# Attention and a mixture of experts in one kernel: one put group for each list, score tiles filled ahead, the block for late rows laid out differently

## The chip, the core and the metric

The kernel runs on one core of a Trainium2 chip. The metric is the device time of one execution in microseconds. Five engines work side by side, each through its own queue of instructions in order: TensorE (PE; its weight loads are shown apart as PEld), VectorE (DVE), ScalarE (ACT), GpSimd (POOL) and SyncE (SP), which here only starts transfers. An engine waits for another one by semaphores.

## The reference

Windowed attention over 8 batches, 8 heads, 576 positions and 64 dimensions gives 4608 rows of 512. Each row then goes to two of eight experts, chosen by noisy gate logits.

```python
scores = scale * np.matmul(q, k.transpose(0, 1, 3, 2))
mask = (rel >= 0) & (rel < window)            # window = 64
scores = np.where(mask, scores, -1000000000.0)
attn = softmax(scores);  x = np.matmul(attn, v)       # rows of 512

logits = x @ w_gate;  noise_scale = np.log1p(np.exp(x @ w_noise))
noisy_logits = logits + noise_scale * noise
top2 = np.argpartition(-noisy_logits, 2, axis=1)[:, :2]
...
for e in range(8):
    for k in range(2):
        mask = top2[:, k] == e
        h = np.maximum(x[mask] @ w1[e], 0.0)          # 512 x 1024
        out[mask] += top2_w[mask, k, None] * (h @ w2[e])
```

(The softmax is written out in the original; `softmax` stands for it here.)

## The kernel before, in words

**Attention, the first 170 us.** 36 units j: nine blocks of 64 positions times four pairs of batches. Units 0 to 3 are the first block, which has no block before it. The loop over j is a pipeline written by hand: in iteration j stand the scores of unit j (L295, later L293), the softmax of j, the transposes of unit j-1 (L329) and the product with v of unit j-2 (L352). The softmax needs a tile `t` of 128 x 512. For later units ScalarE copies scores into it (L303); for units 0 to 3 GpSimd fills it with -8e9 (L305), in `soft_a(j)`. VectorE then copies the permitted scores over it (`soft_max`, L311), takes the maximum (L316), GpSimd subtracts it (L317), and ScalarE takes the exponential (L321). There is one PSUM tile for scores, so the scores of the next unit wait for the copy of this one. Ahead of the loop GpSimd and VectorE build constants (L161 to L596; VectorE's L439 to L596 read some of GpSimd's). `warm(n)` (L150) issues n matmuls on a constant tile whose result nobody reads; the first four units issue four each.

**Lists.** Expert 0 works on all its rows in a simple way. For each expert e from 1 to 7 the generator `top_list(e)` (L639) makes the list of slots: small VectorE steps, three products `tcc` (L670), and then marks and puts. A mark (L682) writes 128 x 512 ones and zeros that tell which lane a row goes to, nine of them for 36 columns. A put (L676) is a matmul of 128 x 50 in bf16 with a mark's columns as weights, 36 for a list, all into one PSUM tile. Marks go through one buffer, `hot`, with room for eight columns, so there are five groups (8, 8, 8, 8, 4), and the puts of a group must be through before its buffer takes new marks. Behind the last put `topa`, `lts` and `ixs` (L694 to L711) are computed, which the gathers and scatters of expert e need.

**Experts.** Each expert has three chunks of rows (384, 448, 384). `up(e, c)` runs eight steps of 12 fp32r matmuls (L857 to L859) that each fill one of three PSUM banks in turn; ScalarE (`hh`, L863) and VectorE (`hl`, L871 and L873; in the last chunk also four `raw` steps, L884 to L887, and `sl`, L878) read the bank. `down(e, c)` (L924 to L926, L979 to L981) writes its rows into `yo`, of which there are three buffers, and GpSimd scatters them to the output with adding DMAs (L900). It also issues the gathers of coming rows (L769). `xy` (L783) has two buffers and holds gathered rows while they are transposed.

**The order of all this.** `spread` lays the side work out over the matmuls of a stage: each part of a list has a start and an end as shares of the stage. `drain(1)` takes one step of the open generators (`pending`), and `due` holds what is to be issued so many calls later. `have(e)` drains until list e is made. List 1 is drained in up(0, 1) and down(0, 1); list 2 in up and down of (0, 2) and in up(1, 0); list e+2 for e = 1 to 5 in down(e, 1), up(e, 2), down(e, 2) and the next chunk's up.

**Late rows.** An expert with more rows than its lists hold needs extra work, `late_rows` (L1256), in the program ahead of the last work item, up(7, 2). Each engine loads the count `nov` into a register (L1259) and branches on it (L1260). With this input the count is zero and the block isn't entered.

## Time and profile before

| | us |
|---|---|
| runs | 1022.56, 1020.47, 1022.13 (median 1022.13) |
| profiled execution | 1023.62 |
| its span | 1021.9 |
| PE busy in the span | 985.5 (96%) |
| DVE busy | 693.6 (68%) |
| POOL busy | 540.7 (53%) |
| ACT busy | 464.7 (45%) |
| mean granted TensorE clock | 0.995 of full speed |

The profiled execution's time is 1.7 us above its span: what lies before the first and behind the last instruction. The durations of instructions below come from this one execution. In a timeline row the first number is the start and the second the length, in us from the span's start; matmuls overlap, so the distance of two starts (the pitch) is what a matmul costs. A bracket at the end says how long the engine had stood idle and what ended it.

### The profile page before, as it was taken

To read this page: it belongs to the slowest core of one execution; us is meant where nothing else is said; L and a number is where in the kernel's file an instruction comes from. 1 tells how busy PE (TensorE), PEld (TensorE's weight loads), DVE (VectorE), ACT (ScalarE), POOL (GpSimd) and SP (SyncE) were. 2 spreads that over 40 slices of the span, in tenths; PEclk is the share of its full clock that TensorE was granted. 3 is DMA by queue.
4 is the path that set the end of the run, shared out by engine and by line. 5 is a ranking of instruction groups with operands and counts; after the bars stand their busy time and mean duration, and the time that the engine had idled before them with its cause. 6 is when DMAs were issued, how large, how long until landed. Compare 5 with 4: busy or idle time off the path is not lost.

```text
span 1021.9 us, 23842 instructions
## 1 busy us (share of the span) xinstructions
PE 985.5 (96%) x9253; PEld 895.1 (88%) x9253; DVE 693.6 (68%) x1716; ACT 464.7 (45%) x1141; POOL 540.7 (53%) x763
## 2 busy tenths in 40 slices
PE   8988989999999999999999999999999999999996
PEld 7776777887888999899999999999999999998995
DVE  6668878755676767766775777678667775467531
ACT  4877775421244435433543254434443543354431
POOL 4432231222776376747575757564667575667411
PEclk9999999999999999999999999999999999999998
DMA  9987897734155135423443334432453344352122
GB/s 326 285 252 219 263 306 275 275 72 100 42 140 113 46 60 132 98 68 63 113 98 87 57 92 99 108 54 81 99 122 55 95 97 109 57 127 52 35 35 31
DMA packets 60667, 123.62 MB, mean 121 GB/s; under 512 B 9728, under 2 KB 9856, under 8 KB 60416
## 3 DMA queue, kind: packets, MB, share of 16 engines
q1 hardware_dynamic: 40816, 83.18, 25.2%
q0 software_dynamic: 19728, 38.82, 21.5%
q8 instruction: 75, 1.23, 0.5%
q14 instruction: 48, 0.39, 0.1%
HBM read 81.59 MB, written 40.37 MB: 119 GB/s over the span
## 4 chain that ended last, share of the span: by engine, by line
PE 74%; DVE 11%; issue 5%; ACT 4%; DMA 4%; POOL 2%; another core or an unknown queue 0%; POOLq 0%; ACTq 0%; DVEq 0%
PE ps_u L857 10%; PE ps_u L859 10%; PE ps_u L858 10%; PE ps_d L924 7%; PE ps_d L925 7%; PE ps_d L926 7%; PE ps_d L979 4%; PE ps_d L981 4%; PE ps_d L980 4%; DMA xg<-xrows,ixs 3%; PE ps_o L352 2%; PE ps_s L293 2%; DVE hot L682 1%; DVE t L311 1%; DVE mx L316 1%
## 5 line engine op out<-in xcount | busy, mean ns | idle before, releaser
L769 POOL DMA_INDIRECT xg<-xrows,ixs x258 | 282.5, 1095 | 65.3 <-issue 52.8
L857 PE MATMUL ps_u<-xh,w1h 128*128 128x384 f32 (+2 forms) x752 | 258.3, 343 | 1.5 <-PEq L1260 1.5
L859 PE MATMUL ps_u<-xh,w1l 128*128 128x384 f32 (+2 forms) x752 | 255.4, 340 | 0.0
L858 PE MATMUL ps_u<-xl,w1h 128*128 128x384 f32 (+2 forms) x752 | 255.4, 340 | 0.0
L863 ACT ACTIVATE hh<-ps_u 128x384 fp32r<-128x384 f32 x188 | 91.7, 488 | 149.6 <-PE ps_u L859 115.4
L900 POOL DMA_INDIRECT out_dram<-yo,lts x67 | 110.9, 1655 | 82.2 <-DVE yo L974 43.0
L857 PEld LDWEIGHTS ps_u<-xh,w1h 128*128 128x128 f32 x752 | 141.2, 188 | 3.5 <-ACT yo L971 1.7
L858 PEld LDWEIGHTS ps_u<-xl,w1h 128*128 128x128 f32 x752 | 141.3, 188 | 1.8
L859 PEld LDWEIGHTS ps_u<-xh,w1l 128*128 128x128 f32 x752 | 141.1, 188 | 1.4
L924 PE MATMUL ps_d<-w2h,hh 128*128 128x512 f32 x352 | 139.2, 395 | 0.6 <-ACT hh L863 0.6
L925 PE MATMUL ps_d<-w2l,hh 128*128 128x512 f32 x352 | 137.6, 391 | 0.3 <-issue 0.3
L926 PE MATMUL ps_d<-w2h,hl 128*128 128x512 f32 x352 | 137.8, 391 | 0.0
L873 DVE SCALAR_TENSOR_TENSOR hl<-ps_u,hh 128x384 fp32r<-128x384 f32 x132 | 73.3, 555 | 94.3 <-ACT hh L863 71.6
L871 DVE SCALAR_TENSOR_TENSOR hl<-ps_u,hh 128x256 fp32r<-128x256 f32 x56 | 23.8, 425 | 106.2 <-ACT raw L869 98.0
L888 ACT ACTIVATE sh<-raw 128x512 fp32r<-128x512 f32 x56 | 35.4, 632 | 128.3 <-DVE raw L887 104.8
L317 POOL TENSOR_TENSOR t<-t,mx 128x512 f32<-128x512 f32 x36 | 37.5, 1043 | 97.8 <-DVE mx L316 73.3
L926 PEld LDWEIGHTS ps_d<-w2h,hl 128*128 128x128 f32 x352 | 66.1, 188 | 14.5 <-DVE hl L873 0.3
L924 PEld LDWEIGHTS ps_d<-w2h,hh 128*128 128x128 f32 x352 | 66.3, 188 | 12.5 <-ACT hh L863 1.0
L925 PEld LDWEIGHTS ps_d<-w2l,hh 128*128 128x128 f32 x352 | 66.2, 188 | 12.2 <-issue 0.7
L768 POOL COPY spacer<-hh 1x1 f32<-1x1 f32 x137 | 33.8, 246 | 69.2 <-ACT hh L863 50.7
L798 ACT ACTIVATE xh<-xy 128x512 fp32r<-128x512 f32 (+2 forms) x67 | 41.2, 615 | 57.7 <-DVE xy L783 52.0
L930 ACT ACTIVATE yo<-ps_d,lts 128x512 f32<-128x512 f32 x35 | 24.1, 689 | 86.4 <-PE ps_d L926 66.8
(277 smaller groups left out, 2068.3 us busy)
## 6 DMA issues: line engine op xcount, KB each, us to landing
stage<-in_w_dram SPq DMA_DIRECT2D x56, 512.0 KB
out_dram<-zero SPq DMA_DIRECT2D x40, 256.0 KB
vw<-in_vx_dram SPq DMA_DIRECT2D x36, 260.0 KB
qc<-in_qT_dram SPq DMA_DIRECT2D x36, 256.0 KB
KW<-in_kT_dram SPq DMA_DIRECT2D x36, 256.0 KB
xrows<-x SPq DMA_DIRECT2D x36, 256.0 KB
xg<-xrows,ixs POOLq DMA_INDIRECT x258
stage<-in_w_dram SPq DMA_DIRECT2D x8, 256.0 KB
```

The source lines that it names most:

```text
L769: nc.gpsimd.indirect_dma_start(out=XG[e, c, t // 4][:, t % 4, :], out_offset=None, in_=XQ[:(DUMP + seen.get((e, c), NT) * 128) * 4], in_of ...
L798: nc.scalar.activation(h, cur[q], AF.Copy)
L857: nc.tensor.matmul(p[:, :n], lhsT=w1h[:, k, fs], rhs=xh[:, k, :n], start=(k == 0), stop=False)
L858: nc.tensor.matmul(p[:, :n], lhsT=w1h[:, k, fs], rhs=xl[:, k, :n], start=False, stop=False)
L859: nc.tensor.matmul(p[:, :n], lhsT=w1l[:, k, fs], rhs=xh[:, k, :n], start=False, stop=(k == KD - 1))
L863: nc.scalar.activation(h, p[:, :main], AF.Relu)
L873: nc.vector.scalar_tensor_tensor(l, p[:, :main], 0.0, h.bitcast(F32), op0=OP.max, op1=OP.subtract)
L900: s = nc.gpsimd.indirect_dma_start(out=out[:DUMP + seen.get((e, c), NT) * 128], out_offset=bass.IndirectOffsetOnAxis(ap=slot(e, c, q)[:m, ...
L924: nc.tensor.matmul(p, lhsT=hh[f][:, sl], rhs=w2h[:, f, :], start=(f == 0), stop=False)
L925: nc.tensor.matmul(p, lhsT=hh[f][:, sl], rhs=w2l[:, f, :], start=False, stop=False)
L926: nc.tensor.matmul(p, lhsT=hl[f][:, sl], rhs=w2h[:, f, :], start=False, stop=(f == KF - 1))
L979: nc.tensor.matmul(p, lhsT=xh, rhs=yh, start=(fresh and i == 0), stop=False, skip_group_check=True)
```

## The change

Three things are edited.

1. **Lists.** The 36 puts of a list now stand in one group. List 1 has a tile of its own for all nine marks (`lone`). Lists 2 to 7 put their marks into five buffers (`marks`): two into `hot`, two into a buffer of `xy`, and two, two and one into the three `yo` buffers. List 2 is marked and put in up(1, 0). Lists 3 to 7 are marked in up(e, 2) with e = 1 to 5; `let`, `last_steps` and `all_done` place the group behind the seventh of its eight steps.
2. **First units.** The tiles `t` of units 0 and 1 are filled ahead of GpSimd's constants, those of units 2 and 3 one iteration ahead, ahead of the subtract of unit 1 and 2. Units 2 and 3 issue one `warm` matmul in place of four.
3. **Late rows.** The register load stands ahead of down(7, 1), and the `If` gets `preferred_fallthrough_block=False`.

```diff
@@ -176,6 +176,15 @@
     nc.vector.tensor_scalar(maskT[:, 1], maskT[:, 0], -1.0, 1.0, op0=OP.mult, op1=OP.add)
 
 
+    EMPTY = {}
+
+    def fill(j):
+        EMPTY[j] = wk.tile([128, 8, 64], F32, name="t")
+        nc.gpsimd.memset(EMPTY[j], -8e9)
+
+    for j in range(2):
+        fill(j)
+
     quarter = consts.tile([128, 1], F32)
     for g in range(4):
         nc.gpsimd.memset(quarter[32 * g:32 * g + 32], float(g))
@@ -296,13 +305,12 @@
                                          start=True, stop=True)
 
     def soft_a(j):
-        t = wk.tile([128, 8, 64], F32, name="t")
-        T[j] = t
         i = j // NP
         if i:
-            nc.scalar.activation(t, ST[j].rearrange("p u g c -> p (u g) c")[:, :, cur_cols(i)], AF.Copy)
+            T[j] = wk.tile([128, 8, 64], F32, name="t")
+            nc.scalar.activation(T[j], ST[j].rearrange("p u g c -> p (u g) c")[:, :, cur_cols(i)], AF.Copy)
         else:
-            nc.gpsimd.memset(t, -8e9)
+            T[j] = EMPTY.pop(j)
 
     def soft_max(j):
         t, p = T[j], ST.pop(j).rearrange("p u g c -> p (u g) c")
@@ -636,6 +644,31 @@
         yield lambda: nc.vector.tensor_reduce(novf[:, E:E + 1], novf[:, 0:E], op=OP.add, axis=AX.X)
         yield lambda: nc.vector.tensor_copy(nov, novf)
 
+    ready, done, LONE = {1}, set(), {}
+
+    def marks(e):
+        if e == 1:
+            return [(0, LONE["p"].tile([128, NT, 128], BF, name="lone"))]
+        x = [exa.tile([128, HALF, 128], BF, name="hot"),
+             exa.tile([128, 4, KD, 32], F32, name="xy", bufs=2).rearrange("p t k c -> p (t k c)")]
+        x += [EXB["p"].tile([128, DM], F32, name="yo", bufs=3) for _ in range(3)]
+        x[1:] = [y.bitcast(BF).rearrange("p (q c) -> p q c", c=128) for y in x[1:]]
+        return [(HALF * k, y) for k, y in enumerate(x)]
+
+    def last_steps(e):
+        return calls[0] >= ready_at[e] + 29
+
+    ready_at = {}
+
+    def let(e):
+        ready.add(e)
+        ready_at[e] = calls[0]
+
+    def all_done(e):
+        ready_at[e] = -100
+        while e not in done:
+            drain(1)
+
     def top_list(e):
         def new(name, shape, dt=F32):
             return gw.tile(shape, dt, name=name, bufs=1)
@@ -675,15 +708,25 @@
             for q in range(a, b):
                 nc.tensor.matmul(got, lhsT=t[:, q - a], rhs=cc[:, q].rearrange("p v k -> p (v k)"),
                                  start=(q == 0), stop=(q == NT - 1))
-        for a in range(0, NT, HALF):
-            b = min(NT, a + HALF)
-            t = exa.tile([128, HALF, 128], BF, name="hot")
-            for q in range(a, b, 4):
-                yield lambda t=t, a=a, q=q: nc.vector.tensor_tensor(
-                    t[:, q - a:q - a + 4], lane[:, None, :].to_broadcast([128, 4, 128]),
-                    ln[:, q:q + 4, None].to_broadcast([128, 4, 128]), op=OP.is_equal)
-            due.append((calls[0] + PUT, lambda t=t, a=a, b=b: put(t, a, b)))
-            yield PUT
+        while e not in ready:
+            yield 1
+        if e > 1:
+            yield 8
+        hot = marks(e)
+        for q in range(0, NT, 4):
+            t = next(x[:, q - a:q - a + 4] for a, x in reversed(hot) if a <= q)
+            yield lambda t=t, q=q: nc.vector.tensor_tensor(
+                t, lane[:, None, :].to_broadcast([128, 4, 128]),
+                ln[:, q:q + 4, None].to_broadcast([128, 4, 128]), op=OP.is_equal)
+        yield PUT if e > 1 else PUT * 3
+        while e > 1 and not last_steps(e):
+            yield 1
+
+        def all_put():
+            for (a, t), b in zip(hot, [a for a, _ in hot[1:]] + [NT]):
+                put(t, a, b)
+            done.add(e)
+        yield all_put
         yield 1
         if not ALL:
             ALL["lt"] = EXB["p"].tile([128, E - 1, HB, 2], I32, name="lts")
@@ -1108,6 +1151,8 @@
             REST[j]()
         on(flip, j - 4)
         on(soft_b, j - 1)
+        if 0 < j < NP - 1:
+            fill(j + 1)
         on(soft_a, j)
         for f in turned.get(j, ())[1:]:
             f()
@@ -1121,7 +1166,7 @@
         if j >= FROM:
             drain_slots(1, gath)
         if j < NP:
-            warm(WARM)
+            warm(WARM if j < 2 else 1)
         on(transp, j - 1)
         on(logits, j - 4)
         if j >= NT:
@@ -1256,8 +1301,7 @@
     def late_rows():
         with ExitStack() as oc:
             ov = oc.enter_context(tc.tile_pool(name="ov", bufs=1))
-            ntot = nc.values_load(nov[0:1, E:E + 1], min_val=0, max_val=2 * OVT)
-            with tc.If(ntot > 0):
+            with tc.If(over["n"] > 0, preferred_fallthrough_block=False):
                 pads()
                 slot_writes()
                 for e in range(E):
@@ -1266,7 +1310,7 @@
                     with tc.For_i(0, ne, 1) as k:
                         overflow(ov, e, k, base)
 
-    later = {}
+    later, over = {}, {}
     for n, (e, c) in enumerate(work):
         nxt = work[n + 1] if n + 1 < len(work) else None
         if not nxt:
@@ -1293,13 +1337,17 @@
         elif c == 1 and e:
             parts0.append((0.0, 0.6, mix_w2(e, 3)))
         if c == 0 and 0 < e < E - 1:
-            parts0.append((0.0, 1.0, [lambda: drain(1)] * 32 + [lambda: have(e + 1)]))
+            if e == 1:
+                let(2)
+            parts0.append((0.0, 1.0, [lambda: drain(1)] * 32 + [lambda: have(e + 1) if e > 1 else all_done(2)]))
         if n == 2:
             parts0.append((0.0, 0.95, gather(*nxt)))
         if last and e < E - 2:
             if e == 0:
                 pending.append(top_list(2))
-            parts0.append((0.0, 1.0, [lambda: drain(1)] * (22 if e else 32)))
+            if e:
+                let(e + 2)
+            parts0.append((0.0, 1.0, [lambda: drain(1)] * (32 if e else 28) + [lambda: all_done(e + 2)] * (e > 0)))
         parts = [(0.0, 1.0, side)] + parts0
         if nxt and n > 2:
             parts.append((0.05, 1.0, later.pop(nxt, None) or gather(*nxt)))
@@ -1318,6 +1366,8 @@
             parts.append((0.0, 0.8, [lambda t=t: zero_out(t) for t in range(*ZEROS[:2])]))
         if n == 1:
             load_w1(1)
+            lone = ExitStack()
+            LONE["p"] = lone.enter_context(tc.tile_pool(name="lone", bufs=1))
             parts.append((0.06, 1.0, [lambda: drain(2)] * 38 + [lambda: have(1)]))
         if n == 0:
             parts.append((0.0, 0.1, halves[SPLIT:]))
@@ -1328,16 +1378,21 @@
             pending.append(top_list(e + 2))
             parts.append((0.0, 1.0, [lambda: drain(1)] * 22))
         if last and e < E - 2:
-            parts.append((0.0, 1.0, [lambda: drain(1)] * (14 if e else 22)))
+            parts.append((0.0, 1.0, [lambda: drain(1)] * (14 if e else 0)))
         if c == 0 and e:
             parts.append((0.0, 1.0, [x for i in range(3) for x in mix_w2(e, i)]))
+        if n == 3:
+            parts.append((0.0, 1.0, [lambda: drain(1)] * 24 + [lambda: have(2)]))
         if 1 < n < len(work) - 2:
             g = gather(*work[n + 2])
             parts.append((0.15, 1.0, g[:SOON]))
             later[work[n + 2]] = g[SOON:]
+        if n == len(work) - 2:
+            over["n"] = nc.values_load(nov[0:1, E:E + 1], min_val=0, max_val=2 * OVT)
         spread(down(e, c), KF * len(tiles(e, c)) - 2 * paired(e, c), *parts)
         if n == 1:
             rt.close()
+            lone.close()
             MIX["p"] = ex.enter_context(tc.tile_pool(name="mix", bufs=1))
             for x in ("th", "tl"):
                 W2[x] = MIX["p"].tile([128, 4, 2, DM], F32R, name=x)
```

The first place is VectorE in up(5, 2), where list 7 is marked: from the last `raw` step of the second up step on, before:

```order
L887 SCALAR_TENSOR_TENSOR raw<-ps_u,raw 128x128
L871 SCALAR_TENSOR_TENSOR hl<-ps_u,hh 128x2x128
L878 TENSOR_TENSOR sl<-raw,sh 128x512
L682 TENSOR_TENSOR hot<-lane,tln 128x512 x2
L873 SCALAR_TENSOR_TENSOR hl<-ps_u,hh 128x384
L884 SCALAR_TENSOR_TENSOR raw<-ps_u,raw 128x128
```

and of the changed kernel from the same instruction on:

```order
L930 SCALAR_TENSOR_TENSOR raw<-ps_u,raw 128x128
L718 TENSOR_TENSOR hot<-lane,tln 128x512 x2
L914 SCALAR_TENSOR_TENSOR hl<-ps_u,hh 128x2x128
L921 TENSOR_TENSOR sl<-raw,sh 128x512
L718 TENSOR_TENSOR xy<-lane,tln 128x512 x2
L718 TENSOR_TENSOR yo<-lane,tln 128x512 x2
L916 SCALAR_TENSOR_TENSOR hl<-ps_u,hh 128x384
L927 SCALAR_TENSOR_TENSOR raw<-ps_u,raw 128x128
```

The two `hot` marks stand one up step earlier, and the `hl` of 128x384 behind them now has four more marks ahead of it instead of two, which go into `xy` and `yo`.

The second place is GpSimd at the start of the program, from its last constants to the subtract of unit 1, before:

```order
L589 IOTA tie 128x7
L591 IOTA place 1x7
L593 IOTA name 1x7
L305 MEMSET t 128x512
L317 TENSOR_TENSOR t<-t,mx 128x512
L305 MEMSET t 128x512
L317 TENSOR_TENSOR t<-t,mx 128x512
L305 MEMSET t 128x512
```

and of the changed kernel, from the fills on (its constants are the same, and stand between these rows):

```order
L173 AFFINE_SELECT other<-ones 128x128
L183 MEMSET t 128x512 x2
L190 MEMSET quarter 32x1 x4
L405 AFFINE_SELECT tri<-ones 128x128
L410 IOTA rev 128x8
```

```order
L597 IOTA tie 128x7
L599 IOTA place 1x7
L601 IOTA name 1x7
L325 TENSOR_TENSOR t<-t,mx 128x512
L183 MEMSET t 128x512
L325 TENSOR_TENSOR t<-t,mx 128x512
L183 MEMSET t 128x512
L325 TENSOR_TENSOR t<-t,mx 128x512 x4
```

Two fills stand ahead of all constants from `quarter` on, and the other two stand one subtract earlier than they did.

The third place is TensorE at the end of down(7, 1), where the block for late rows begins; before:

```order
L979 MATMUL ps_d<-th,hh 128x256
L980 MATMUL ps_d<-tl,hh 128x256
L981 MATMUL ps_d<-th,hl 128x256
L1259 TENSOR_LOAD nov
L1260 COMPARE_AND_BRANCH
L1264 TENSOR_LOAD nov
```

and of the changed kernel there:

```order
L1022 MATMUL ps_d<-th,hh 128x256
L1023 MATMUL ps_d<-tl,hh 128x256
L1024 MATMUL ps_d<-th,hl 128x256
L1304 COMPARE_AND_BRANCH
L1304 UNCONDITIONAL_BRANCH
L1308 TENSOR_LOAD nov
```

The register load has left the place (it stands behind the last matmul of up(7, 1)), and where one branch on the compare stood there is now a compare and an unconditional branch behind it.

## Rows read from the trace of the kernel before

**Rows 1.** The page's chain that ended last: share of the span by engine.

```profile
PE 74%; DVE 11%; issue 5%; ACT 4%; DMA 4%; POOL 2%; another core or an unknown queue 0%; POOLq 0%; ACTq 0%; DVEq 0%
```

**Rows 2.** Waits of TensorE: line, waited for, us in total, times, longest us.

```profile
PE ps_g L676 <- DVE hot L682: 4.3, 9, 1.5
```

**Rows 3.** Waits of VectorE, the same columns.

```profile
DVE t L311 <- POOL t L305: 3.4, 3, 1.6
```

**Rows 4.** Timeline of TensorE in up(5, 2), list 7: start us, us, instruction, [idle before].

```profile
780.43 0.34 PE L857 MATMUL ps_u<-xh,w1h 128*128 128x384 f32 x1
...
786.18 0.38 PE L676 MATMUL ps_g<-tcc,hot 128*128 128x50 bf16 x8
786.40 0.42 PE L857 MATMUL ps_u<-xh,w1h 128*128 128x384 f32 x1
786.66 0.34 PE L858 MATMUL ps_u<-xl,w1h 128*128 128x384 f32 x1
...
797.21 0.28 PE L676 MATMUL ps_g<-tcc,hot 128*128 128x50 bf16 x4
797.79 0.27 PE L676 MATMUL ps_g<-tcc,hot 128*128 128x50 bf16 x4 [0.30 <-DVE hot L682]
```

**Rows 5.** Timeline of TensorE: list 1 in down(0, 1), list 2 in down(0, 2).

```profile
234.87 0.39 PE L926 MATMUL ps_d<-w2h,hl 128*128 128x512 f32 x1
235.41 0.27 PE L676 MATMUL ps_g<-tcc,hot 128*128 128x50 bf16 x4 [0.15 <-DVE hot L682]
236.01 0.27 PE L676 MATMUL ps_g<-tcc,hot 128*128 128x50 bf16 x4 [0.33 <-DVE hot L682]
...
278.62 0.40 PE L926 MATMUL ps_d<-w2h,hl 128*128 128x512 f32 x1
280.50 0.27 PE L676 MATMUL ps_g<-tcc,hot 128*128 128x50 bf16 x4 [1.49 <-DVE hot L682]
281.70 0.27 PE L676 MATMUL ps_g<-tcc,hot 128*128 128x50 bf16 x4 [0.93 <-DVE hot L682]
```

**Rows 6.** Timeline of VectorE in up(5, 2).

```profile
788.54 0.42 DVE L871 SCALAR_TENSOR_TENSOR hl<-ps_u,hh 128x256 fp32r<-128x256 f32 x1 [1.41 <-ACT raw L869]
...
789.53 1.28 DVE L682 TENSOR_TENSOR hot<-lane,tln 128x512 bf16<-128x512 bf16 x2
790.73 0.55 DVE L873 SCALAR_TENSOR_TENSOR hl<-ps_u,hh 128x384 fp32r<-128x384 f32 x1
...
792.16 0.29 DVE L887 SCALAR_TENSOR_TENSOR raw<-ps_u,raw 128x128 f32<-128x128 f32 x1
```

**Rows 7.** Timeline of GpSimd: last scatter of down(5, 1).

```profile
784.26 1.58 POOL L900 DMA_INDIRECT out_dram<-yo,lts  x1 [0.27 <-issue]
```

**Rows 8.** Stretch of up(5, 2): length, busy us of each engine, PEclk, DMA share, GB/s.

```profile
790.00:795.00 5.00, 5.00 (x37) 4.84 (x36) 3.49 (x10) 1.71 (x4) 3.19 (x5) 1.00 0.16 43
```

**Rows 9.** Timeline of VectorE at the start.

```profile
4.87 1.07 DVE L449 CAST acc<-padi 128x10 f32<-128x10 int32 x1
...
6.10 0.71 DVE L311 COPY_PREDICATED t<-mcur,ps_s 128x512 f32<-128x512 uint32 x1
...
15.30 0.73 DVE L311 COPY_PREDICATED t<-mcur,ps_s 128x512 f32<-128x512 uint32 x1 [0.71 <-POOL t L305]
...
19.06 0.73 DVE L311 COPY_PREDICATED t<-mprev,ps_s 128x512 f32<-128x512 uint32 x1 [1.40 <-ACT t L303]
```

**Rows 10.** Timeline of TensorE at the start.

```profile
9.38 0.65 PE L329 MATMUL ps_t<-ident,p 128*128 128x128 f32 x4 [0.73 <-ACT p L321]
```

**Rows 11.** Timeline of TensorE around the block for late rows.

```profile
977.45 0.28 PE L981 MATMUL ps_d<-th,hl 128*128 128x256 f32 x1
979.25 0.41 PE L857 MATMUL ps_u<-xh,w1h 128*128 128x384 f32 x1 [1.52 <-PEq L1260]
```

**Rows 12.** Instructions of lines 1259 and 1260: engine, operation, count, ns, start us.

```profile
L1259 PEldq TENSOR_LOAD <-nov x1: 489/489/489, 974.8 to 974.8; - x1
...
L1260 PEldq COMPARE_BRANCH  x1: 3566/3566/3566, 975.4 to 975.4; - x1
```

## Prediction

> **What bounds the kernel now.** I read the chain of waits first. TensorE carries 74% of it and VectorE 11% [rows 1], so a microsecond counts only where TensorE stands still, or where it does something that the change removes. The second view is therefore the waits of TensorE: the put of a list waits 4.3 us in all, in nine places [rows 2]. The third is VectorE's wait for the filled score tiles at the start, 3.4 us in three places [rows 3]. The timelines around these places, and around the block for late rows, give the terms below. The profiled execution took 1023.62 us (span 1021.9 and 1.7 around it); the median of the runs is 1022.13, so the sum, made against the profile, is lowered by 1.5 at the end. A measurement of this kernel can tell about 0.2%, 2.0 us, from no change.
>
> **The put in one group (all seven lists).** One group of eight puts takes 786.18 to 786.40, 0.0275 a matmul; the first fp32r matmul behind it has its successor 0.26 later [rows 4] where the pitch is 0.174 (33 matmuls from 780.43 to 786.18 [rows 4]). A change of kind costs 0.086. Five groups become one: 4 x 0.086 = 0.34 a list, less whatever the new place costs.
>
> **List 1.** The matmul at 234.87 would be followed at 235.10, by the 0.23 pitch around it; the put starts at 235.41. Its four matmuls end at 235.52, the next four start at 236.01 [rows 5]. Lost: 0.31 + 0.49 = 0.80. Afterwards nine marks run one after the other on VectorE into a tile of their own, 0.60 each (789.53 to 790.73 for two [rows 6]); the first stood complete before the put at 235.41, so nine are through by 240.2, while the put comes about where the third group was, near 243. Nothing waits: gain 0.80 + 0.34 = 1.1 (0.3 if the put still met an unfinished mark, 1.3 at best).
>
> **List 2.** The marks began while TensorE was already due: 278.62 should be followed at 278.85 and is followed by a put at 280.50; 280.61 should be followed at once and is followed at 281.70 [rows 5]. Lost: 1.65 + 1.09 = 2.74, plus 0.34. Now all marks and the put lie in the up stage of the next chunk, where VectorE also cuts weights; some 5.4 us of marks make the hidden layer's low halves later there, and I charge 0.1 for one bank that comes late. Term 3.0, bounds 1.5 (1.5 of that queue reaching TensorE) and 3.1.
>
> **Lists 3 to 7, by list 7.** Here a wait goes and another comes. Gone: 4 x 0.086, and the wait of the third group's second half, 797.79 less 797.21 less 0.11 = 0.47 [rows 4]: 0.81. New: the fourth step's work on VectorE is queued behind six marks instead of two. From the order: two marks go into the `hot` buffer in VectorE's free time before 788.54; then come hl, sl, and now four marks (xy, yo) where two stood [rows 6]. The hl of the fourth step, 790.73 before, starts 2 x 0.60 = 1.2 later, 791.93, and its last raw step, 792.16 to 792.45 before [rows 6], ends at 793.65. The seventh up step writes the PSUM bank that this step reads (three banks in turn). Without put groups between, TensorE reaches it at 780.43 + 6 x 12 x 0.1736 = 792.93. It waits until about 793.70: 0.77. The three last marks end near 795.4; the seventh step ends at 795.78, so the put finds all marks done. Net 0.81 - 0.77 = 0.04 a list, 0.2 for five. Bounds: +0.81 each (4.1) if the bank comes in time, -0.7 each if the last marks also delay the step behind.
>
> The yo marks write buffers that the scatters of the chunk before still read. The last is issued at 784.26 [rows 7], and over 790 to 795 the DMA engines' share is 0.16 [rows 8], so they are through by then; the first yo mark into a late buffer is due near 793.6. I cost this wait at nothing. Behind a mark that waits, VectorE's whole queue stands (hl, raw, sl), and TensorE behind that.
>
> **First units.** One tile period before is (15.30 - 6.10) / 3 = 3.07 [rows 9], and a fill stands in it each time, because POOL makes it only behind the subtract of the unit before. Added: two fills of 0.5 stand ahead of POOL's constants, which VectorE's first operations read; the conversion at 4.87, 1.07 long [rows 9] beside POOL's work, has room to shrink. First copy 6.65 instead of 6.10. The second needs only its scores and VectorE's copy and maximum: 8.1. The third waits for scores that stand on TensorE behind the transposes of unit 0 (9.38, 0.65 long [rows 10]; 0.55 later, so scores until 11.2): 11.2. The fourth by the same steps about 13.9, against 15.30; the unit behind it 17.7 against 19.06 [rows 9]. I take 1.3, near the middle: at most 3.36, all three waits [rows 3]; at least -1.0, both fills added and nothing won. From there the shift holds as long as the loads come early enough, and the warm matmuls left out stood beside VectorE's chain, so they add nothing.
>
> **Late rows.** TensorE's last matmul before the block starts at 977.45, its next at 979.25; by the pitch there, 0.12, it was due at 977.57 [rows 11]: 1.68 lost. Its sequencer runs ahead, with the register load at 974.8, 2.65 before the start of that last matmul; it spends 489 ns on the load and 3566 ns on the branch [rows 12]. The load moves ahead of a down stage, where that lead hides it (if it doesn't, it costs the same 0.5 there). The branch: the order shows that the compare now falls through, but on an unconditional branch over the same block. So one far jump is left, and the gain is the load, 0.5. Bounds: 0 and 1.68. [...]
>
> **Sum.** 1.1 + 3.0 + 0.2 + 1.3 + 0.5 = 6.1. The end of the kernel follows TensorE's end, so it moves along. Profile 1023.62 - 6.1 = 1017.5; against the median 1022.13 - 6.1 = 1016.0.
>
> **Rivals.**
> 1. The bank in lists 3 to 7 comes in time (VectorE's chain is shorter than I have it, or the marks slip into its gaps). For it: VectorE idles before 788.54. Against it: the order puts four marks directly ahead of the hl that the bank needs. Time: five more times 0.77, 1016.0 - 3.9 = 1012.1.
> 2. Slower: in each of lists 3 to 7 a yo mark waits for a scatter of the chunk before, and VectorE's queue behind it holds TensorE. For it: the buffers are the same three, and a scatter needs its issue and its landing. Against it: nothing much moves on the DMA engines after 790 [rows 8]. The other terms are worth 5.9; the change is a loss once TensorE waits 1.2 a list more than I have it, that is, if the scatter issued at 784.26 lands after about 795. Landing at 796.2 is 2.4 a list, 12 in all: 1028.
> 3. Part of the gain is given back outside the lists: the start is held by loads (full DMA engines) so that the 1.3 vanish, and the cuts in list 2's new place cost 1.5. Then 6.1 - 1.3 - 1.5 = 3.3: 1018.8; with the bank of lists 3 to 7 dearer by 0.3 each, 1020.3, inside the 2 us.
> [...]
>
> **How the numbers follow.** Forecast case 0.54, rival 1 0.12, rival 2 0.14, rival 3 0.15, rival 4 0.05. Faster by over 0.2% (below 1020.1): the forecast case, rivals 1 and 4 and two thirds of rival 3, 0.81. Within 0.2%: a third of rival 3 (0.05) and the mild end of rival 2 (0.03), 0.08. Slower: the rest of rival 2, 0.11. The range goes from rival 1 with a little of rival 4, 1011.5, up to 1021, which leaves out most of rival 2. Range of the forecast case alone: 1013.5 to 1018.5.
>
> **What would show it.** In the changed profile: no wait of the put for a mark; 36 puts in some 1.0 us; a wait of about 0.7 before the seventh up step of the last chunk of experts 1 to 5, with VectorE's raw as its releaser; the copy of unit 4 near 17.7; one register load of `nov` on TensorE ahead of the last but one down stage, and a branch still of 3 us or more before the last up stage, with a pause near 1.2 before its first matmul. Wrong it is if VectorE shows idle time before yo marks with a DMA as releaser, if the copies at the start still come 3 us apart, or if TensorE's gap before the last up stage is 1.7 or near 0.

## The result, and the profile after

The changed kernel took 1026.57 us (median of 6 runs, 1024.69 to 1033.24) against 1022.15 (6 runs, 1020.47 to 1024.56) for the kernel before: ratio 1.0058, interval 1.0037 to 1.0079, so 4 to 8 us slower, where 6 us faster had been forecast. The profiled execution took 1026.58 with a span of 1024.8, against 1023.62 and 1021.9.

The waits of TensorE, answering to [rows 2]; columns as there:

```profile
PE ps_o L360 <- issue: 9.6, 9, 2.1
PE ps_u L900 <- issue: 5.7, 1, 5.7
PE ps_u L900 <- DVE raw L930: 3.0, 5, 0.6
```

The put's wait for marks (4.3 us) is gone. In its place there is a wait for `raw`, five times, as forecast. But the largest single wait is new: 5.7 us before a first matmul of an up stage, for nothing that the profile shows.

List 7 in up(5, 2), TensorE and then VectorE, answering to [rows 4, 6]:

```profile
790.82 0.44 PE L900 MATMUL ps_u<-xh,w1h 128*128 128x384 f32 x1 [0.57 <-DVE raw L930]
...
793.01 0.38 PE L709 MATMUL ps_g<-tcc,hot 128*128 128x50 bf16 x8
793.24 0.36 PE L709 MATMUL ps_g<-tcc,xy 128*128 128x50 bf16 x8
793.44 0.67 PE L709 MATMUL ps_g<-tcc,yo 128*128 128x50 bf16 x20
```

```profile
787.84 1.29 DVE L718 TENSOR_TENSOR yo<-lane,tln 128x512 bf16<-128x512 bf16 x2
789.04 0.55 DVE L916 SCALAR_TENSOR_TENSOR hl<-ps_u,hh 128x384 fp32r<-128x384 f32 x1
...
790.48 0.29 DVE L930 SCALAR_TENSOR_TENSOR raw<-ps_u,raw 128x128 f32<-128x128 f32 x1
```

The seventh up step waits 0.57 for the `raw` step that starts at 790.48, behind the two yo marks of 787.84 and the `hl` of 789.04. The 36 puts follow in one run from 793.01, the next up matmul starts at 793.95, and they wait for nothing.

The first units, answering to [rows 9]: VectorE's copies.

```profile
6.21 0.73 DVE L319 COPY_PREDICATED t<-mcur,ps_s 128x512 f32<-128x512 uint32 x1
...
7.82 0.73 DVE L319 COPY_PREDICATED t<-mcur,ps_s 128x512 f32<-128x512 uint32 x1 [0.16 <-PE ps_s L304]
...
10.93 0.75 DVE L319 COPY_PREDICATED t<-mcur,ps_s 128x512 f32<-128x512 uint32 x1
...
13.45 0.70 DVE L319 COPY_PREDICATED t<-mcur,ps_s 128x512 f32<-128x512 uint32 x1
...
17.25 0.73 DVE L319 COPY_PREDICATED t<-mprev,ps_s 128x512 f32<-128x512 uint32 x1 [1.31 <-ACT t L311]
```

No fill ends an idle time any more, and unit 4 came 1.8 earlier (17.25 for 19.06). Later in attention it is lost again; TensorE near 44 us, and the stretch behind it (length, busy us of each engine, granted clock, DMA share, GB/s):

```profile
39.78 1.10 PE L302 MATMUL ps_s<-KW,qc 64*64 64x128 f32 x32
...
41.41 0.85 PE L360 MATMUL ps_o<-vw,pt 64*64 64x65 f32 x41
44.33 0.58 PE L360 MATMUL ps_o<-vw,pt 64*64 64x65 f32 x23 [2.07 <-issue]
...
46.26 1.99 PE L302 MATMUL ps_s<-KW,qc 64*64 64x128 f32 x32
```

```profile
46.00:48.00 2.00, 2.00 (x39) 1.80 (x37) 1.03 (x3) 1.01 (x3) 0.73 (x1) 0.50 0.95 247
```

TensorE stops in the middle of one run of 64 equal matmuls, 41 done and 23 to go, for 2.07 us, with "issue" as the releaser. Behind the pause the granted clock is 0.50, and the 32 score matmuls take 1.99 us where the 32 at 39.78 took 1.10.

The block for late rows, answering to [rows 11, 12]: TensorE, its sequencer's instructions of that line (count, ns min/median/max, first and last start), and two stretches behind it.

```profile
974.56 0.28 PE L1024 MATMUL ps_d<-th,hl 128*128 128x256 f32 x1
980.49 0.69 PE L900 MATMUL ps_u<-xh,w1h 128*128 128x384 f32 x1 [5.65 <-issue]
980.97 0.52 PE L901 MATMUL ps_u<-xl,w1h 128*128 128x384 f32 x1
```

```profile
L1304 PEldq COMPARE_BRANCH  x2: 95/2674/5252, 971.9 to 975.2; - x2
...
L1304 PEldq EVENT_SEMAPHORE  x2: 51/51/51, 974.9 to 975.0; - x2
```

```profile
980.40:985.00 4.60, 4.51 (x16) 4.51 (x17) 0.00 (x0) 0.33 (x1) 0.00 (x0) 0.58 0.22 41
985.00:990.00 5.00, 5.00 (x31) 5.00 (x30) 2.06 (x6) 1.81 (x5) 0.09 (x1) 1.00 0.00 2
```

From the end of the matmul of 974.56 to 980.49 nothing runs. The compare takes 95 ns at 971.9, ahead of the matmuls as planned. Then come two semaphore instructions, at 974.9 and 975.0: right behind the end of the last matmul (974.56 + 0.28 = 974.84). Only at 975.2 does the unconditional branch start, and it takes 5252 ns. After the pause the clock is down: 0.58 on average to 985.

**Where the time went**, by the starts of TensorE's stages in the two timelines: attention ends 2.64 later (first up matmul 182.11, now 184.75); down(0, 1) is 1.27 shorter, down(0, 2) 4.37, up(1, 0) 0.12; down(1, 0) is 0.31 longer; from up(1, 2) to up(7, 0) 0.12 is won; from the start of down(7, 1) to that of up(7, 2) 4.14 is lost, and in up(7, 2) 1.76 more. TensorE ends 3.00 later. Two of these differences say little of the change: attention's lies within the spread between profiles, and most of down(0, 2)'s is peculiar to the one profile of before; the experiments show both.

### The profile page after: what moved, and what is told of

Its sections match the earlier page's. It is cut to its first block, busy times and chain, and to the rows that moved or that the text cites. A ratio compares the mean times of both kernels' runs of the same rounds, so it can differ in the third digit from the quotient of the medians.

```text
span 1024.8 us, 23817 instructions
## 1 busy us (share of the span) xinstructions
PE 984.9 (96%) x9241; PEld 898.7 (88%) x9241; DVE 691.9 (68%) x1716; ACT 465.3 (45%) x1141; POOL 550.4 (54%) x763
## 4 chain that ended last, share of the span: by engine, by line
PE 80%; DVE 7%; issue 5%; DMA 4%; ACT 2%; POOL 1%; POOLq 0%; ACTq 0%; DVEq 0%
PE ps_u L900 11%; PE ps_u L902 11%; PE ps_u L901 11%; PE ps_d L967 7%; PE ps_d L969 7%; PE ps_d L968 7%; PE ps_d L1022 4%; PE ps_d L1024 4%; PE ps_d L1023 4%; PE ps_o L360 3%; DMA xg<-xrows,ixs 3%; PE ps_s L302 2%; PE ps_t L337 2%; PE ps_g L266 2%; PE ps_g L279 2%
## 5 line engine op out<-in xcount | busy, mean ns | idle before, releaser
L811 POOL COPY spacer<-hh 1x1 f32<-1x1 f32 x137 | 39.0, 285 | 66.3 <-ACT hh L906 48.0
```

## The experiments

Times vary by several us from run to run of one program (before: 1017.4 to 1026.05 in the 35 runs beside e1 to e4), so a difference below 1.5 us is read from stages and not from the total. The stages outside attention, down(0, 2) and the late rows repeat to 0.1 to 0.3 us (down(0, 0) to 0.5). Five such readings from the timelines, in us:

| kernel | first up matmul | down(0, 2) | up(1, 2) to up(7, 0) | last matmul before up(7, 2) to its first | up(7, 2) |
|---|---|---|---|---|---|
| before | 182.11 | 20.73 | 547.08 | 1.80 | 16.74 |
| changed | 184.75 | 16.36 | 546.96 | 5.93 | 18.50 |
| e1_lists | 183.93 | 16.36 | 547.16 | 1.92 | 16.72 |
| e2_first | 180.14 | 16.98 | 547.05 | 1.60 | 16.72 |
| e3_late | 182.75 | 16.99 | 547.07 | 4.95 | 19.58 |
| e4_late_load | 187.67 | 16.99 | 547.04 | 1.20 | 16.72 |
| e5_no_kv | 177.48 | 16.99 | 547.11 | 1.65 | 16.74 |
| e6_fill | 182.95 | 16.99 | 547.09 | 1.84 | 16.74 |
| e7_late_end | 185.07 | 16.99 | 547.05 | 0.12 | 16.66 |
| e8_mend | 185.46 | 16.36 | 542.62 | 2.01 | 16.72 |
| e9_best | 184.10 | 16.36 | 542.62 | 1.11 | 16.75 |
| e10_best_fill | 186.81 | 16.36 | 542.54 | 1.44 | 16.74 |
| e11_small | 185.54 | 16.99 | 547.08 | 0.58 | 16.72 |
| e12_small_late | 185.22 | 16.98 | 547.18 | 1.02 | 16.75 |
| e13_no_kv | 176.60 | 22.31 | 546.93 | 1.77 | 16.72 |
| e14_no_kv_fill | 175.93 | 20.68 | 547.07 | 1.78 | 16.72 |
| e15_no_kv_first | 175.43 | 22.19 | 547.10 | 1.81 | 16.72 |

With the first units as before and all loads, the first up matmul came at 182.11 to 187.67 in nine profiles (184.65 on average), with the fills ahead at 180.14 to 186.81 in four (183.66). The 2.64 between the profiles of before and of the changed kernel lie within that spread.

**The parts apart.**

```diff
 e1: lists as changed; first units and late rows as before
 e2: first units as changed; the rest as before
 e3, on before:
+        if n == len(work) - 2:
+            over["n"] = nc.values_load(nov[0:1, E:E + 1], ...)
-            with tc.If(ntot > 0):
+            with tc.If(over["n"] > 0, preferred_fallthrough_block=False):
 e4: as e3, but
+            with tc.If(over["n"] > 0):
```

> Only the lists' part of the change; first units and late rows as before. Theory A (from the two traces: stage starts of TensorE moved 5.5 us earlier between up(0, 1) and down(7, 1), the losses lie in attention and at the late rows): 1022.15 - 5.5 = 1016.6, and no trace of the late loss (gap of 1.7 us before the last up stage). Theory B (the lists' marks in the yo buffers also cost something that shows only at the end): no faster than 1019.

Measured 1019.1 against 1020.38: ratio 0.9981 (0.9964 to 0.9998), 1.9 us faster. Theory A had the sign and not the size; the stages show why: 3.7 of the 5.5 was the long down(0, 2) of the one profile of before (20.73, where eight other profiles of the same code have 16.98 or 16.99). TensorE's waits in e1:

```profile
PE ps_o L352 <- issue: 8.6, 7, 3.1
PE ps_u L892 <- DVE raw L922: 3.1, 5, 0.7
...
PE ps_u L892 <- PEq L1295: 1.6, 1, 1.6
```

> Only the first units' part (fills ahead and one warm matmul in place of four in units 2 and 3). Theory A (TensorE's pauses in the middle of equal matmuls, with nothing that the profile shows as releaser, are instruction fetches that stand behind full DMA engines; they come at fixed places of the instruction stream and are longer in the changed kernel, 2.07 us at 44 us and a lower clock after it): unit 8 is 1.4 us earlier, and the first up stage starts 1 to 3 us later than before, 1023 to 1025. Theory B (these pauses vary by chance from run to run and the change has no part in them): unit 8 1.4 us earlier and the gain kept, 1020.8.

Measured 1020.83: ratio 1.0007 (0.9985 to 1.0029). Unit 8 came 1.5 earlier, and the total shows nothing of it. The pauses stand 12 matmuls later in the instruction stream than before (runs with 36, 29, 16 and 3 matmuls to go, where the profiles with the old stream, of before, e1, e3 and e6, have 48, 41, 28 and 15), which fits fixed places in that stream: the page counts 12 matmul records fewer (9253 before, 9241 after), each with a weight load, as each matmul of these runs has one. Their lengths vary from profile to profile.

> Only the late rows' part (register load earlier, the other order of the blocks). Theory A (in the new order TensorE's sequencer first runs two semaphore instructions, which wait until its matmuls are through, and only then starts the far jump; nothing covers the jump): the gap before the last up stage is 5 to 6 us instead of 1.7 and the clock falls after it; 1022.15 + 4 to 6 = 1026 to 1028. Theory B (the long jump of 5.25 us was chance): a gap of 1.2 to 3.6, 1021.6 to 1024.

Measured 1025.1: ratio 1.0046 (1.0029 to 1.0062), 4.7 us slower. TensorE's sequencer in e3, whose last matmul before the block ended at 974.65, and in e4, whose last ended at 979.47:

```profile
L1259 PEldq COMPARE_BRANCH  x2: 95/2181/4267, 971.7 to 975.0; - x2
...
L1259 PEldq EVENT_SEMAPHORE  x2: 51/51/51, 974.7 to 974.8; - x2
```

```profile
L1259 PEldq EVENT_SEMAPHORE  x2: 51/51/51, 980.1 to 980.3; - x2
...
L1259 PEldq COMPARE_BRANCH  x1: 3555/3555/3555, 976.5 to 976.5; - x1
```

In e3 the semaphores stand at 974.7 and 974.8, behind the matmuls' end, and a jump of 4267 ns follows uncovered; the granted clock is 0.50 from 980 to 985. In e4 the jump comes first, at 976.5, beside 3 us of queued matmuls, and the semaphores at 980.1 and 980.3 take 51 ns each. Theory A holds.

> Only the register load moved ahead of down(7, 1); the order of the blocks as before. Theory A (the far jump then starts 0.5 us earlier and is covered by queued matmuls as before): gap 1.2 us, 1021.6. Theory B (the load itself is the trouble, wherever the branch goes): gap of 5 us as in the changed kernel, 1026.

Measured 1019.78: ratio 0.9992 (0.9974 to 1.0009), not to be told from no change; the gap is 1.20 instead of 1.80, as forecast for the load alone. In the table the gap is 1.60 to 2.01 in the nine profiles with the load and the branch at their old place, and 1.11 to 1.44 in the three with the load alone moved (e4, e9, e10).

**What the pauses in attention are.**

```diff
 e5, on before:
-        if 0 < j < NT - 3:
+        if 0 < j < NT - 3 and j + 3 < 8:
             load_k(j + 3)
-        if j + NP < NT:
+        if j + NP < 8:
             load_v(j + NP)
```

> The kernel before, with the loads of k and v left out from the third block on (the attention then works on stale keys and values; nothing else differs, and TensorE's instructions are the same). Theory A (TensorE's pauses in attention are instruction fetches behind full DMA engines): the pauses at the fixed places of the kernel before (before the last 54, 48, 35, 28, 22, 15, 9, 2 matmuls of a product with v) shrink from the 30th us on to a few tenths, from 6 to 10 us in all to under 3; the first up stage starts 4 to 7 us earlier than the 182 to 188 of four profiles of this attention, and the runs spread less. Theory B (they are waits for the keys or values themselves, or for the buffers): they also go, but places move and TensorE then waits for other engines. Theory C (sequencer or branch cost that has nothing to do with the DMA engines): the same pauses, first up stage at 182 to 188.

Measured 1015.29: ratio 0.9929 (0.9905 to 0.9953). Its waits of this kind:

```profile
PE ps_o L352 <- issue: 2.6, 4, 0.8
...
PE ps_t L329 <- issue: 0.5, 1, 0.5
```

With less to load (DMA share 0.48 between 30 and 80 us, where before has 0.84), these pauses come to 3.1 us where the same attention had 8.6 and 1.9 in e1; attention ended at 177.48, and the five runs span 3.0 us against 7.3 for the 24 of before.

Two things in the traces show what TensorE waits for. The first is the places. Counted along TensorE's queue (weight loads, matmuls and its semaphore instructions), the pauses of before stand at instructions 1218, 1985, 2242, 2754, 3009, 3266, 3777 and 4034, and those of e5 at 1473, 2242, 2754, 3010 and 3265: multiples of 256 apart, to within one. In the 17 profiles this holds for 174 of the 177 pauses of over 0.15 us in attention that have "issue" as their releaser. So the places did not move in e5, although fewer matmuls were left behind them (48, 27, 13 and 6 to go, for 48, 28, 15 and 9): its queue has 25 semaphore instructions fewer (129 for 154), and nothing is left of theory B.

The second is a DMA queue that the page lists by itself (packets, MB, share of 16 engines):

```profile
q8 instruction: 75, 1.23, 0.5%
```

Its packets have 16,384 bytes (64 for each instruction, if one packet holds the 256 between two places: an estimate), and in attention one follows the other after some 5 us. In 171 of the 174 pauses TensorE went on 1.2 to 1.6 us after such a packet had landed, in the other three after 0.8 to 1.1. In the changed kernel's pause of 2.07 us the packet ran from 40.84 to 42.87, and TensorE went on at 44.33. By these places and packets theory A holds: TensorE waits for its own instructions. In sum these pauses are 5.7 to 13.2 us in the thirteen profiles with all loads and 1.9 to 3.4 in the four without (e5, e13 to e15). The packets take 1.0 to 1.1 us on average in both kinds; how the loads delay them is not shown.

> Only the fills ahead, with all four warm matmuls kept, so TensorE's instructions are those of before. Theory A (the fills win 1.4 us at unit 8 and the fetch pauses, at their old places, are the same on average): 1020.4 - 1.4 = 1019.0, unit 8 about 33.2. Theory B (a start earlier by 1.4 us is given back in fetch pauses, since DMA engines are full until some 60 us whatever TensorE does): 1020.4, with longer pauses.

```diff
 e6: fills as in the change; in the loop
             warm(WARM)
```

Measured 1021.79: ratio 0.9996 (0.998 to 1.0013). The fills alone win nothing that can be measured.

**Other places for the block, and the distance.**

```diff
 e7, on before: the call moved behind the loop
-        if not nxt:
-            late_rows()
...
+    late_rows()
     ex.close()
 e11 (on e4) and e12 (on e3):
-                for e in range(E):
+                for e in range(1):
```

> The kernel before with the block for late rows moved behind the last work item. Theory A (the far jump then stands behind TensorE's last matmul and beside the last scatters' way to memory, some 5 us after GpSimd issues them): TensorE runs from down(7, 1) into up(7, 2) without a gap (1.7 us won), and the end is not later: 1018.7. Theory B (GpSimd's load, branch and semaphores at the end come on top, 4 to 8 us): 1023 to 1027.

Measured 1021.37: ratio 0.9999 (0.9979 to 1.0018). The gap is gone (0.12), but the end came 12.3 us behind the start of TensorE's last matmul instead of 10.5 (1008.42 and a span of 1020.7; before 1011.41 and 1021.9; 9.8 to 10.6 in the other profiles). It moves the price to the end.

> The kernel with the register load moved and the old order of the blocks, and the block for late rows cut to expert 0 (the late rows of the other experts are left out; with this input there are none): some 13 of TensorE's 90 rows of the block are left. Theory A (the jump's 3.4 to 3.9 us on TensorE are a fixed price of a taken branch there, whatever its distance): 3.4 to 3.9 again. Theory B (they grow with the distance jumped): 1 to 2, and the gap before the last up stage goes.

> The late rows' part of the change with the same small block (late rows of experts 1 to 7 left out). Theory A (the semaphores ahead of the jump wait for the last matmul, and the jump has a fixed price): the semaphores again stand within 0.1 us behind the last matmul's end, the jump takes 4 to 5 us, the gap is 4.7 to 6 from start to start. Theory B (the price grows with the distance): semaphores at the same place, the jump 1 to 2 us, the gap 2 to 3.

Measured 1021.3 (ratio 0.9985, 0.9966 to 1.0004) and 1022.16 (0.9991, 0.9959 to 1.0024). The rows of e11 and e12, of the same line:

```profile
L1259 PEldq EVENT_SEMAPHORE  x2: 51/51/51, 977.0 to 977.2; - x2
...
L1259 PEldq COMPARE_BRANCH  x1: 389/389/389, 974.0 to 974.0; - x1
```

```profile
L1259 PEldq COMPARE_BRANCH  x2: 95/218/342, 973.8 to 977.1; - x2
...
L1259 PEldq EVENT_SEMAPHORE  x2: 51/51/51, 976.8 to 977.0; - x2
```

The jump takes 389 and 342 ns where it took 3555 and 4267, so it has no fixed price. What goes with the price stands in the packets of q8. In all fifteen profiles with the whole block one of them starts 1.0 to 2.1 us after the jump, and the jump ends 1.3 to 1.5 us after that packet landed (changed kernel: jump at 975.18, packet 977.31 to 979.10, end 980.43). In e11 and e12 no packet falls into the jump: both jumps are shorter than theory B had it (1 to 2 us). That the price grows step by step with the distance is not shown; the two distances show a long jump with a packet and a short one without. The semaphores stand within 0.05 us behind the last matmul's end in both (976.96 in e11, 976.79 in e12): that part of theory A holds. The gaps are 0.58 and 1.02, less than the 2 to 3 of theory B for e12, and not gone as it had it for e11.

**Lists 3 to 7 with the marks laid into gaps.**

```diff
 e8, on e1:
-        if e > 1:
+        if e == 2:
             yield 8
         hot = marks(e)
         for q in range(0, NT, 4):
+            if e > 2 and q in (8, 16, 24):
+                yield q // 8
```

> The lists' part alone, with the marks of lists 3 to 7 laid into VectorE's gaps: two, two, one, one, three over the up steps instead of two, four, three. Theory A (the seventh up step waits because four marks stand ahead of the hl and raw of the fourth step): that wait, 0.6 in each of five lists, goes; from up(1, 2) to up(7, 0) TensorE is 3.0 us shorter than with the lists' part alone (547.16), 544.2; time 1019.1 - 3.0 = 1016.1. Theory B (the bank is late for another reason, or a yo mark now waits for a scatter): less than 1 us shorter, or longer.

Measured 1015.35: ratio 0.9923 (0.99 to 0.9946), about 7.9 us faster than before. VectorE in up(5, 2) of e8, and TensorE's two longest waits:

```profile
783.35 0.69 DVE L712 TENSOR_TENSOR yo<-lane,tln 128x512 bf16<-128x512 bf16 x1
783.95 0.55 DVE L910 SCALAR_TENSOR_TENSOR hl<-ps_u,hh 128x384 fp32r<-128x384 f32 x1
...
785.39 0.29 DVE L924 SCALAR_TENSOR_TENSOR raw<-ps_u,raw 128x128 f32<-128x128 f32 x1
```

```profile
PE ps_o L352 <- issue: 7.7, 7, 2.2
PE ps_u L894 <- PEq L1297: 1.7, 1, 1.7
```

One mark instead of four stands ahead of the fourth step's `hl`; its last `raw` step starts at 785.39, before TensorE needs the bank, and the wait for `raw` is not among TensorE's waits any more. The five lists are 4.5 us shorter (547.16 to 542.62), more than the 3.0 forecast, which was the idle time in the brackets. Counted by the pitch the one wait costs more: in up(5, 2) of e1 the first matmul of the seventh step starts 0.91 behind its predecessor and the next one 0.28 behind it, where the pitch is 0.17, so 0.84 are lost for 0.7 or less of idle time; no other step of that stage lost anything, and the five up stages with a list are 0.87 to 0.95 shorter in e8.

> The lists' part with the marks laid into VectorE's gaps, and the register load moved ahead of down(7, 1) with the old order of the blocks; first units as before. Theory A (the gains add, since the stages after attention repeat to some hundredths of a us): 1015.35 - 0.6 = 1014.7, gap before the last up stage 1.2 from start to start. Theory B (the load or the jump costs more in this order of work): 1016 or above.

> The same with the fills ahead and all four warm matmuls kept. Theory A (the 1.4 us won at the start are kept on average): 1.4 below the same kernel without them, 1013.3. Theory B (they are given back in fetch pauses, so that nothing is left that can be told from no change): within 0.7 of it.

Measured 1015.16 (ratio 0.9932, 0.9905 to 0.9959) and 1014.27 (0.9919, 0.989 to 0.9948). Both beat the kernel before and the changed one; against e8 and each other nothing can be told.

**The fills once more, with shorter pauses.**

> The kernel before with the loads of k and v left out from the third block on, again, as the base of the next two: 1015.3 as before, all runs within 3 to 4 us.

> The same with the fills ahead, warm matmuls as before (k and v from the third block on left out). Theory A (the fills' 1.4 us are kept through attention and were only hidden under the pauses' chance): 1.4 below the base, 1013.9. Theory B (they are given back also here, at a later stage of attention that is paced by something else than TensorE): within 0.5 of the base.

> The same with the whole first units' part, fills ahead and one warm matmul in place of four in units 2 and 3 (k and v from the third block on left out). Theory A (fewer warm matmuls cost nothing, they only move the places of the pauses): as with the fills alone, 1013.9. Theory B (the moved places of the pauses are worse ones): 1 to 2 above the fills alone.

Before took 1027.36 beside these three, more than beside the others, and the base 1018.91 instead of 1015.3 (its down(0, 2) is 22.31), so only comparisons with this before count: ratios 0.9922 (0.9904 to 0.994), 0.9925 (0.9908 to 0.9941) and 0.9922 (0.9904 to 0.9939). Neither edit moves the total. In the profiles the fills are 1.9 ahead at unit 8 (0.7 of it stood already at the first copy, 6.22 against 6.95) and 2.2 at unit 15, then 0.7 from unit 18 on, behind pauses of 0.80 and 0.28 that the base doesn't have there. Both are waits for instructions, at multiples of 256 as in e5. One profile of each does not show whether such pauses always take the gain back, so that stays open; by e6's interval it is below about 2 us.

## Why the prediction was wrong

- **Late rows: the step that decided.** "So one far jump is left, and the gain is the load, 0.5" took for granted that the jump still starts while matmuls are queued. The load was worth 0.6 (e4). But in the new order two semaphore instructions stand ahead of the jump and behind TensorE's last matmul (974.7 and 974.8 in e3, its end 974.65); the jump of 4267 ns starts only then, no matmul runs beside it, and the granted clock is 0.50 from 980 to 985. Measured -4.7 for +0.5 (e3). In the trace of before the two semaphore instructions stood behind the branch; I read the branch's 3.57 us and not what stands beside it. Rival 4, in which that jump goes (0.05 of the chances and a little of the range), is shown by no run: over the whole block the jump took 3.4 to 5.3 us on TensorE in all fifteen profiles.
- **List 2.** "Lost: 1.65 + 1.09 = 2.74" was read from an execution in which ScalarE and VectorE had been late before the marks. VectorE's last `hl` but one ahead of them in before, ScalarE's `hh` that it reads, and the same `hl` in e2, whose list 2 is the same:

```profile
272.84 0.56 DVE L873 SCALAR_TENSOR_TENSOR hl<-ps_u,hh 128x384 fp32r<-128x384 f32 x1 [3.02 <-issue]
```

```profile
272.32 0.49 ACT L863 ACTIVATE hh<-ps_u 128x384 fp32r<-128x384 f32 x1 [4.08 <-PE ps_u L859]
```

```profile
267.94 0.56 DVE L881 SCALAR_TENSOR_TENSOR hl<-ps_u,hh 128x384 fp32r<-128x384 f32 x1 [0.54 <-ACT hh L871]
```

  VectorE stood 3.02 us for an `hh` that was itself late; the marks and both waits of [rows 5] for list 2 followed from that. With list 2 unchanged, down(0, 2) took 16.98 or 16.99 in eight profiles and 20.68 to 22.31 in four (before and e13 to e15); with the change it took 16.36 in five of five. Against the eight the term is 0.6 from down(0, 2) and 0.1 from up(1, 0), less the 0.3 by which down(1, 0) grew: 0.4 and not 3.0. Whether the new place also avoids the long case isn't shown. The chain behind a wait has to be followed until it reaches something that repeats.
- **List 1.** Forecast 1.1, measured 1.27 (down(0, 1)). Right.
- **Lists 3 to 7.** Forecast 0.2 in sum with a new wait of 0.77 each; measured 0.12 in the profile (-0.08 in e1), with a wait of 0.57 idle in up(5, 2), or 0.73 counted by the pitch as the forecast counts it (the matmul ahead of the one at 790.82 starts at 789.92, and the pitch is 0.17). Right, by the mechanism named. No yo mark waited for a scatter: VectorE's only wait ahead of one (us in total, times, longest) is

```profile
DVE yo L718 <- issue: 0.2, 1, 0.2
```

  so the cost of nothing stood, and rival 2 didn't happen.
- **First units.** Forecast 1.3 at unit 4 and a shift that holds. Unit 4 gained 1.8, unit 8 1.4; the shift didn't hold: e2, e6 and e14 show no gain in time. "From there the shift holds as long as the loads come early enough" left out that TensorE also waits for its own instructions, which come by DMA (q8, 75 packets of 16,384 bytes before), and that its waits for them differ by more (5.7 to 13.2 us in all) than the shift is worth. "So they add nothing", of the warm matmuls left out, was wrong as well: from the first copy to that of unit 4 it is 12.96 in before, 11.83 with the fills alone (e6, e10, e14) and 11.04 to 11.18 where units 2 and 3 also issue one warm matmul in place of four (changed, e2, e15).
- **The sum.** Parts measured apart: -1.9 (e1), +0.7 (e2), +4.7 (e3), together +3.5 within wide bounds; the whole measured +5.9 (3.8 to 8.1). By stages, leaving out attention, which says nothing below its spread: -1.3 for list 1, -0.4 for list 2, -0.1 for lists 3 to 7, and 4.1 + 1.8 for the late rows, together +4.1. Slower was forecast with 0.11, on a mechanism that did not occur.

## What to carry to other kernels

Give a far branch queued work beside it (jumps of 3555 and 4267 ns made a gap of 1.20 us beside 3 us of queued matmuls in e4, and of 4.95 beside none in e3): look at what the block ahead of the jump waits for, not only at how many jumps there are. Before a wait is counted as a gain, see whether it repeats in a second execution, or follow its chain to a cause that the program sets. When work is spread into an engine's queue, put it into the gaps ahead of the instruction that another engine needs: the same nine marks of each list in another order were worth 4.5 us over five lists. And a pause that sits at the same distance, again and again, in an engine's instruction stream, with no releaser, is worth counting in instructions: here the distance was 256.

## What the runs showed of the hardware

- TensorE waited for its own instructions in attention: 174 of 177 pauses with no releaser stand multiples of 256 instructions apart, 0.2 to 3.1 us each and another length in each execution, and 171 end 1.2 to 1.6 us after a packet of 16,384 bytes of the instruction queue q8 had landed. In all they are 5.7 to 13.2 us with all loads (DMA share 0.84 between 30 and 80 us in before) and 1.9 to 3.4 with the loads of k and v left out from the third block on (0.48 in e5).
- A pause of 2.07 us in attention was followed by a granted clock of 0.50 until about 49 us, and the pauses of 4.7 and 5.7 us before up(7, 2) by up(7, 2) of 19.58 and 18.50 us instead of 16.7.
- A jump over the whole block took 3.4 to 5.3 us on TensorE, with one packet of q8 in each of fifteen profiles, and ended 1.3 to 1.5 us after the packet landed; over an eighth of the block it took 0.34 and 0.39, with none.
- In the profiles of before and of e13 to e15 ScalarE's last two `hh` of up(0, 2) start 2.8 to 4.3 and 5.1 us after the last matmul of their steps; in the other thirteen profiles all eight start 0.37 after it. TensorE's records show nothing in these steps. I did not find out what sets the four apart. The profiles of e13 to e15 come from one chip and those of the other experiments from three others; which chip gave the profile of before is not on record.
